# Sliding-window attention and an ELU feed-forward: finer first loads, clears in two steps, another order of the first transfers, and a split last row block

## Chip, cores and metric

The kernel runs on one core of a Trainium2 chip. The metric is the device time of the whole kernel in microseconds (us). The engines are called as in the profile: PE (TensorE, the matrix engine; PEld is its weight load), DVE (VectorE), ACT (ScalarE), POOL (GpSimd) and SP (SyncE). POOL and SP also issue DMA transfers.

## What is computed

The reference takes q, k and v of 8 batches, 8 heads, 576 positions and 64 columns. Each query position attends to the keys at most 32 positions away. The attention output of all heads, 4608 rows of 512 columns, goes through a feed-forward layer with 2048 hidden columns and an ELU between the two matrices.

```python
scores = scale * np.matmul(q, k.transpose(0, 1, 3, 2))       # scale = 1/sqrt(64)
scores = np.where(np.abs(pos[:, None] - pos[None, :]) <= 32, scores, -1e9)
attn = softmax(scores)
x = (attn @ v).transpose(0, 2, 1, 3).reshape(4608, 512)
h = x @ w_in                                                  # 512 -> 2048
g = np.where(h > 0, h, np.exp(np.minimum(h, 0)) - 1)
out = g @ w_out                                               # 2048 -> 512, fp32
```

## The kernel before

Work is cut into 36 **pairs** of 64-row query blocks (i = 0 to 35, 128 rows of x each, 4.5 pairs to a batch) and into 10 **tiles** t of the feed-forward: tiles 0 and 1 hold two pairs (256 rows), the other eight hold four (512 rows). All operations are named, with the engine that does them:

- `L b nm half`: POOL issues a transfer that loads half of the heads of q or k of batch b as bf16 (288 KB). `LV b qb`: the same for a 128-row window of v. `WI c` and `WO c`: a quarter of `w_in` or `w_out` (512 KB). `ID` and `MS` are no transfers: POOL makes the identity matrix and the band masks.
- `T b nm hp` and `E b nm hp` (batches 0 to 2): PE transposes two heads of q or k into PSUM (18 matmuls of 64x64), and ACT copies the result to `qT` or `kT`. In batch 0 DVE does the k copies.
- `SV`: copies within `vw` (`copy_v`) that build the odd windows of v; DVE does them in batches 0 and 1.
- `QK i`, `SM i`, `MK i`, `AV i g`, `RN i g`: scores on PE, exponential on ACT (PSUM `psS`, one buffer), masking on DVE, product with v on PE in two head groups g, normalisation on DVE.
- `XT i` and `X i`: x of pair i is transposed for the feed-forward. Pairs 0 to 7 go over PE (`XT`, 4 matmuls into `psT`) and ACT (`X`, the copy); all later ones are a DMA transpose that SP issues. `psT` has one buffer, which the T of batches 1 and 2 and all XT share. So T, its copy E, XT and its copy X go round one after another, in whatever order PE's queue has them.
- `H t fo` (PE, PSUM `psH` with three buffers), `EX`, `FF`, `GG` (exponential on ACT, then on DVE or ACT, then DVE): one 128-column block of the hidden layer of a tile. `Y t c part` (PE), `YC` (ACT copy), `OUT` (SP transfer): four parts of the second product for 128 output rows.

The order on every engine is written by a planner when the program is built (`class Plan`). Each operation has an engine, an assumed duration, a rank and its dependencies; at each step the engine that is free takes the ready operation of lowest rank. The program that comes out is a fixed queue for each engine: an instruction that waits holds all behind it. POOL's first transfers are an exception, since the list `RING` gives their order by hand. At most eight of POOL's transfers are under way: each one waits for the eighth before it. All of them go through one DMA queue.

Before the plan is run, DVE clears parts of three `vw`, two `kT` and two `pm` buffers (15 memsets), which stand at the head of its queue. The last 128 output rows (tile 9, c = 3) are computed as 16 matmuls of 512 columns; ACT copies one half of the columns and DVE the other, and each half is stored by a transfer of its own.

Of the kernel before, what the change touches and what calls it, by code (L numbers as in the profile page):

```python
# [8 lines left out]
FP32 = mybir.dt.float32  # L9
BF16 = mybir.dt.bfloat16  # L10
# [146 lines left out]
def kernel(  # L157
# [19 lines left out]
    HP = H // 2  # L177
    PR = 96
    TPP = S // PR
    TPW = S // QB  # L180
    NWB = 3
    KW = S + 2 * WIN
# [36 lines left out]
            for b in range(B) for nm in "qk" for hp in range(HP)}  # L219

    def make_masks():
        mf = ep.tile([128, 4, QB], FP32, name="mf", tag="e")
# [26 lines left out]

    def wide(b):  # L250
        return b < NWB

    def load_qk(b, nm, half):
        src = {"q": q, "k": k}[nm]
        src = src[b, half * HP:(half + 1) * HP]
        if half == 0:
            live[nm, b] = bfp.tile(
                [128, HP, TPW * D] if wide(b) else [PR, H, TPP * D], BF16,
                name="bf", tag="bf")
        t = live[nm, b]  # L260
        if wide(b):
            t = t[:, half * HP // 2:(half + 1) * HP // 2]
            src = src.rearrange("(n a) (p t) d -> (a p) n (t d)", a=2, t=TPW)
        else:
            t = t[:, half * HP:(half + 1) * HP]
            src = src.rearrange("h (p t) d -> p h (t d)", t=TPP)
        nc.gpsimd.dma_start(out=t, in_=src)  # L267

    def T(b, nm, hp):
        src = live[nm, b]  # L270
        n = 2 * hp + (nm == "k")
        pool, tag = (psH_p, "psH") if b == 0 and n % 4 else (psT_p, "psT")
        pt = pool.tile([128, TPW, QB] if wide(b) else [128, TPP, PR], BF16,
                       name=tag, tag=tag)
        live["T", b, nm, hp] = pt
        if wide(b):
            for j in range(TPW):
                for a in (0, QB):
                    nc.tensor.transpose(pt[a:a + QB, j, :],  # L279
                                        src[a:a + QB, hp, j * D:(j + 1) * D],  # L280
                                        ident[a:a + QB, a:a + QB])
            return
        for j in range(TPP):
            nc.tensor.transpose(pt[:, j, :],
                                src[:, 2 * hp:2 * hp + 2, j * D:(j + 1) * D],
                                ident[0:PR, 0:PR])

    def E(b, nm, hp):
        pt = live.pop(("T", b, nm, hp))
        if nm == "k":  # L290
            dst = kT[b % NKB][:, hp, WIN:WIN + S]
        else:
            dst = qT[b % NKB][:, hp, :]
        dst = dst.rearrange("c (p t) -> c p t", t=TPW if wide(b) else TPP)
        src = pt.rearrange("c t p -> c p t")
        if EVAC[b, nm, hp] == "ACT":
            nc.scalar.copy(dst, src)  # L297
        else:
            nc.vector.tensor_copy(dst, src)  # L299
# [123 lines left out]
    def X(i):  # L423
# [5 lines left out]
        dst = xts[t][:, :, c * 128:(c + 1) * 128]  # L429
        if i >= NPX:  # L430
            nc.sync.dma_start_transpose(dst, xs)
            return
# [55 lines left out]

    def Y(t, c, part):
        if part == 0:  # L490
            pool, nm = ypool(t, c)
            ys[t, c] = pool.tile([128, DM], FP32, name=nm, tag=nm)
        ps = ys[t, c]
        for fo in range(YQ * part, YQ * part + YQ):
            nc.tensor.matmul(ps, lhsT=gs[t][:, fo, c * 128:(c + 1) * 128],  # L495
                             rhs=w_out_sb[:, fo, :],
                             start=(fo == 0), stop=(fo == NFO - 1))

    def YC(t, c):
        y = yp.tile([128, DM], FP32, name="y", tag="y")  # L500
        if (t, c) == yseq[-1]:
            nc.scalar.copy(y[:, 0:DM // 2], ys[t, c][:, 0:DM // 2])
            nc.vector.tensor_copy(y[:, DM // 2:DM], ys.pop((t, c))[:, DM // 2:DM])
        else:
            nc.scalar.copy(y, ys.pop((t, c)))  # L505
        ys[t, c] = y

    def OUT(t, c):
        r = (tiles[t][0] + c) * 128
        y = ys.pop((t, c))  # L510
        if (t, c) == yseq[-1]:
            nc.sync.dma_start(out[r:r + 128, 0:DM // 2], y[:, 0:DM // 2])
            nc.scalar.dma_start(out[r:r + 128, DM // 2:DM], y[:, DM // 2:DM])
        else:
            nc.sync.dma_start(out[r:r + 128, :], y)

# [11 lines left out]
    YS1 = 2  # L528
    NPX = 8

    P = Plan({"SP": 0.8, "ACT": 0.8, "POOL": 0.8, "DVE": 6.0})
    FC = 512
# [19 lines left out]
    def prank(i):  # L552
        return PER * tiles[where[i][0]][0] + PER * (i - tiles[where[i][0]][0]) - LEAD[i >= NLEAD] - 16

    SVOF = {}
    NV3 = 4
    LQ0, LQD = 64.0, 2.4
    XQ0, XQD = 38.0, 3.0
# [7 lines left out]
        ('L', 0, 'q', 1),  # L566
        ('L', 0, 'k', 1),
        ('ID',),
        ('LV', 0, 0),
        ('LV', 0, 2),  # L570
        ('MS',),
        ('LV', 0, 4),
        ('LV', 0, 6),
        ('WI', 0),
        ('WI', 1),
        ('L', 1, 'q', 0),
        ('L', 1, 'k', 0),
        ('WI', 2),
        ('LV', 0, 8),
        ('WI', 3),  # L580
        ('L', 1, 'q', 1),
        ('L', 1, 'k', 1),
        ('WO', 0),
        ('LV', 1, 0),
        ('WO', 1),
        ('LV', 1, 2),
        ('WO', 2),
        ('LV', 1, 4),
        ('WO', 3),
        ('L', 2, 'q', 0),  # L590
        ('L', 2, 'k', 0),
        ('LV', 1, 6),
        ('LV', 1, 8),
        ('L', 2, 'q', 1),
# [17 lines left out]
    for b in range(B):  # L612
        need = prank(b * NQB // 2)
        for j in range(NTB) if b >= XB else ():
            for nm in "kq":
# [7 lines left out]
                else:  # L623
# [10 lines left out]
                     dma=0.5, wt=0.05, solo=0.4, lat=LATX)  # L634
        for half in range(2) if b < XB else ():
            for nm in ("q", "k"):
                n = ("L", b, nm, half)
                deps = []
                if b >= 2:
                    deps += [("T", b - 2, nm, hp) for hp in range(HP)]  # L640
                P.op(n, "POOL", 0.75, RING.index(n) - 999, deps,
                     lambda b=b, nm=nm, half=half: load_qk(b, nm, half),
                     dma=1.5 if wide(b) else 1.7, wt=0.1, soft=ring(n))
        deps = []
# [3 lines left out]
        for qb in range(0, NQB, 2):  # L648
            x = need - LQ0 + LQD * (qb / 2 + (NV3 if b == XB else 0))
            P.op(("LV", b, qb), "POOL", 0.9,  # L650
                 RING.index(("LV", b, qb)) - 999 if b < XB else x,
                 deps + (gate(x) if b >= XB else []),
                 lambda b=b, qb=qb, g=gate(x) if b >= XB else []: load_v(
                     b, qb, g),
                 dma=1.3 if 0 < qb < NQB - 1 else 1.0, wt=0.04,
                 soft=ring(("LV", b, qb)))
# [15 lines left out]
        for hp in range(HP) if b < XB else ():  # L672
            for nm in ("q", "k"):
                n = hp * 2 + (nm == "k")
                deps = [("L", b, nm, hp // 2), ("ID",)]
                m = n - (4 if b == 0 else 1)
                if m >= 0:
                    deps.append(("E", b, "qk"[m % 2], m // 2))
                elif b:
                    deps.append(("E", b - 1, "k", HP - 1))  # L680
                P.op(("T", b, nm, hp), "PE", 0.5 if wide(b) else 0.3, need - 36 + 4 * n, deps,
                     lambda b=b, nm=nm, hp=hp: T(b, nm, hp))
                deps = [("T", b, nm, hp)]
                if b >= NKB:
# [3 lines left out]
                     lambda b=b, nm=nm, hp=hp: E(b, nm, hp))  # L688

    P.op(("ID",), "POOL", 0.6, RING.index(("ID",)) - 999, [],  # L690
         lambda: make_identity(nc, ident), soft=ring(("ID",)))
# [9 lines left out]
    for i in range(NPAIR):  # L701
# [17 lines left out]
        P.op(("SM", i), "ACT", 1.05, r, deps, lambda i=i: SM(i))  # L719
        deps = [("SM", i), ("MS",)]  # L720
        if i >= 2:
# [28 lines left out]
        if t >= 2:  # L750
            deps.append(("H", t - 2, NFO - 1))
        if i < NPX:
            if i:
                deps.append(("X", i - 1))
# [32 lines left out]
    for n, (t, c) in enumerate(yseq):  # L787
        for part in range(NQ):
            r = (PER * (tiles[t][0] + tiles[t][1])
                 + 2 * YSP.get(t, 1) * (c * NQ + part) + 1)  # L790
            deps = [("GG", t, fo) for fo in range(YQ * part, YQ * part + YQ)]
            deps.append(("WO", part * YQ * NWC // NFO))
            if part:
# [3 lines left out]
            elif c == 1:  # L797
                deps.append(("RN", NPAIR - 1, 1))
            P.op(("Y", t, c, part), "PE", 0.86, r, deps,
                 lambda t=t, c=c, part=part: Y(t, c, part))  # L800
        deps = [("Y", t, c, NQ - 1)]
        if n >= 3:
# [6 lines left out]
    with tc.manual_schedule():  # L809
        for t in vw:  # L810
            nc.vector.memset(t[0:WIN, 0, :, 0:D], 0.0)
            nc.vector.memset(t[128 - WIN:128, NQB - 1, :, 0:D], 0.0)
            nc.vector.memset(t[:, 0:NQB:2, :, D:VW], 1.0)
        for t in kT:
            nc.vector.memset(t[:, :, 0:WIN], 0.0)
            nc.vector.memset(t[:, :, WIN + S:KW], 0.0)
        for t in pm:
            nc.vector.memset(t[:, :, QB:2 * QB], 0.0)
        P.run()
# [28 lines left out]
```

The softmax here doesn't subtract the row's maximum and nothing guards it: scores larger than these inputs give would overflow.

## Time and profile before

| | |
|---|---|
| median of 5 runs | 325.17 us (324.61 to 326.88) |
| the profiled execution's own time | 324.61 us |
| its span | 322.6 us |
| PE busy | 303.9 us (94%) |
| DVE, ACT, POOL busy | 211.6, 196.5, 107.8 us |
| start of the first H (tile 0) | 24.52 us |
| start of the first H of 512 rows (tile 2) | 67.50 us |
| end of PE's last matmul | 318.98 us |

The profiled execution is the fastest of the five, 0.56 us below the median. Its span is the time between the first and the last recorded event; 2.0 us of its time lie around it. An engine's busy time in a slice is the union of its instructions; PE's ends are modelled. In a timeline row the bracket gives how long the engine was idle before the instruction, and what ended that.

### The profile page before, as it was taken

How to read it: one execution, taken by the hardware profiler on the slowest of the kernel's cores; microseconds unless marked ns; L12 is line 12 of the kernel's file. 1: busy time of each engine (PE TensorE's matmuls, PEld its weight loads, DVE VectorE, ACT ScalarE, POOL GpSimd, SP SyncE). 2: the span in 40 equal slices, each digit the busy share in tenths (PEclk: the TensorE clock that was granted, in tenths of full speed). 3: DMA queues.
4: the chain of work that ended last, by engine and by line, in shares of the span. 5: the costliest groups of instructions: out<-in, count | busy, mean ns of one | idle time of the engine just before them, and what ended most of it. 6: DMA issues, size and time to landing. Idle time of an engine off the chain costs nothing.

```text
span 322.6 us, 7515 instructions
## 1 busy us (share of the span) xinstructions
PE 303.9 (94%) x2896; PEld 160.1 (50%) x2896; DVE 211.6 (66%) x500; ACT 196.5 (61%) x333; POOL 107.8 (33%) x203
## 2 busy tenths in 40 slices
PE   1589998899999999999999999999999999999995
PEld 1467666555555444444444444444444454444442
DVE  4586687668888777777666666666666665454500
ACT  3258987778756555555666666666666665556511
POOL 8945447935456645154456434000000000000000
PEclk9999999999999999999999999999999999999999
DMA  7999999999999999999999999532221111000021
GB/s 100 134 203 203 197 196 189 155 169 179 138 148 230 161 170 184 198 142 158 163 131 163 189 150 159 105 83 68 61 60 59 50 53 49 33 35 33 33 98 65
DMA packets 140371, 41.04 MB, mean 127 GB/s; under 512 B 125360, under 2 KB 135856, under 8 KB 140336
## 3 DMA queue, kind: packets, MB, share of 16 engines
q0 software_dynamic: 91872, 18.36, 76.9%
q1 hardware_dynamic: 48320, 22.08, 34.2%
q8 instruction: 22, 0.36, 0.5%
q10 hardware_dynamic: 144, 0.13, 0.1%
q14 instruction: 13, 0.11, 0.1%
HBM read 36.70 MB, written 9.44 MB: 143 GB/s over the span
## 4 chain that ended last, share of the span: by engine, by line
PE 83%; DMA 8%; POOL 4%; ACT 1%; issue 1%; DVE 1%; ACTq 0%; POOLq 0%
PE psH L452 36%; PE psY L495 35%; PE psO L405 5%; DMA vw<-in_v_dram 4%; DMA w_in_sb<-in_moe_w_in_dram 4%; PE psS L372 3%; POOL bf L267 1%; PE psS L495 1%; PE psO L495 1%; PE psT L495 1%; POOL vw L336 1%; PE psT L279 1%; ACT kT L297 1%; POOL w_in_sb L538 0%; PE psT L435 0%
## 5 line engine op out<-in xcount | busy, mean ns | idle before, releaser
L452 PE MATMUL psH<-xt,w_in_sb 128*128 128x512 bf16 (+1 forms) x640 | 148.3, 360 | 0.5 <-DVE g L481 0.5
L460 ACT ACTIVATE e<-psH 128x512 f32<-128x512 f32 (+1 forms) x160 | 88.3, 554 | 88.1 <-PE psH L452 87.4
L495 PE MATMUL psY<-w_out_sb,g 128*128 128x512 bf16 x528 | 134.2, 379 | 0.2 <-DMA w_out_sb<-in_moe_w_out_dram 0.2
L452 PEld LDWEIGHTS <-w_in_sb 128*128 128x128 bf16 x640 | 59.5, 98 | 56.6 <-issue 1.0
L495 PEld LDWEIGHTS <-g 128*128 128x128 bf16 x576 | 52.7, 98 | 56.5 <-issue 0.5
L478 DVE SCALAR_TENSOR_TENSOR g<-f,psH 128x512 bf16<-128x512 bf16 (+1 forms) x72 | 45.0, 624 | 33.9 <-ACT f L470 33.8
L472 DVE TENSOR_SCALAR f<-e 128x512 bf16<-128x512 f32 (+1 forms) x88 | 37.7, 428 | 36.4 <-ACT e L460 36.3
L481 DVE TENSOR_TENSOR g<-psH,f 128x512 bf16<-128x512 f32 (+1 forms) x88 | 56.5, 642 | 3.2
L470 ACT ACTIVATE f<-e 128x512 bf16<-128x512 f32 (+1 forms) x72 | 41.9, 582 | 2.2
L380 ACT ACTIVATE pu<-psS 128x1024 bf16<-128x1024 f32 x36 | 36.7, 1020 | 7.4 <-PE psS L372 6.4
L336 POOL DMA_DIRECT2D vw<-in_v_dram x40 | 33.6, 842 | 15.7 <-issue 3.5
L405 PEld LDWEIGHTS <-pm 128*128 128x128 bf16 x576 | 27.1, 100 | 13.9 <-DVE xs L420 0.5
L308 POOL COPY scr<-g 1x1 bf16<-1x1 bf16 x73 | 14.9, 204 | 53.6 <-DVE g L481 44.1
L420 DVE TENSOR_TENSOR xs<-psO,rc 128x256 bf16<-128x256 f32 x68 | 28.9, 424 | 2.4
L405 PE MATMUL psO<-vw,pm 128*128 128x65 bf16 x544 | 28.4, 195 | 0.3 <-DVE xs L420 0.3
L393 DVE TENSOR_TENSOR pm<-pu,masks 128x512 bf16<-128x512 bf16 x72 | 27.0, 417 | 1.5 <-ACT pu L380 1.5
L317 POOL DMA_DIRECT2D bf<-in_k_dram x25 | 20.9, 838 | 7.3 <-issue 5.2
L317 POOL DMA_DIRECT2D bf<-in_q_dram x25 | 20.9, 838 | 5.2 <-issue 4.1
L505 ACT COPY y<-psY 128x512 f32<-128x512 f32 x33 | 18.8, 570 | 5.3 <-PE psY L495 5.3
L372 PEld LDWEIGHTS <-kT 64*128 64x128 bf16 (+1 forms) x640 | 12.1, 102 | 15.0 <-issue 11.9
L372 PE MATMUL psS<-qT,kT 64*128 64x64 bf16 (+1 forms) x640 | 16.9, 199 | 2.5 <-DVE kT L299 1.4
L418 DVE RECIPROCAL rc<-psO 128x4 f32<-128x4 f32 x68 | 12.3, 181 | 9.9 <-PE psO L405 9.4
(47 smaller groups left out, 99.0 us busy)
## 6 DMA issues: line engine op xcount, KB each, us to landing
out_dram<-y SPq DMA_DIRECT2D x35, 256.0 KB, 2.9
vw<-vw SPq DMA_DIRECT2D x12, 260.0 KB, 7.0
vw<-in_v_dram POOLq DMA_DIRECT2D x24, 128.0 KB, 7.2
bf<-in_k_dram POOLq DMA_DIRECT2D x20, 128.0 KB, 6.7
bf<-in_q_dram POOLq DMA_DIRECT2D x20, 128.0 KB, 6.2
w_in_sb<-in_moe_w_in_dram POOLq DMA_DIRECT2D x4, 512.0 KB, 11.0
w_out_sb<-in_moe_w_out_dram POOLq DMA_DIRECT2D x4, 512.0 KB, 13.9
bf<-in_q_dram POOLq DMA_DIRECT2D x6, 288.0 KB, 10.4
```

Of the source, the lines that this page charges most:

```text
L317: nc.gpsimd.dma_start(out=live["N", nm, b][0:n, j, :].rearrange("p (h d) -> p h d", d=D), in_=src[128 * j:128 * j + n])
L336: nc.gpsimd.dma_start(out=vt[r:r + hi - lo, qb, :, 0:D], in_=vb[lo:hi])
L372: nc.tensor.matmul(psS[p0:p1, h % 2, s, hp, :], lhsT=kT[b % NKB][base:base + 64, hp, c:c + p1 - p0], rhs=rhs, start=True, stop=True)
L380: nc.scalar.activation(pu, live.pop(("S", i)), AX.Exp, scale=SCALE)
L405: nc.tensor.matmul(o[:, j, :], lhsT=p[:, h, s * QB:s * QB + 128], rhs=vw[b % NVB][:, qb, h, :], start=(s == 0), stop=(s == 1))
L452: nc.tensor.matmul(ps, lhsT=w_in_sb[:, do, fo * 128:(fo + 1) * 128], rhs=xts[t][:, do, :], start=(do == 0), stop=(do == NDO - 1))
L460: nc.scalar.activation(e, ps, AX.Exp)
L470: nc.scalar.activation(f, e, AX.Relu, bias=1.0, scale=-1.0)
L472: nc.vector.tensor_scalar(f, e, -1.0, 0.0, ALU.add, ALU.min)
L478: nc.vector.scalar_tensor_tensor(gs[t][:, fo, :], f, -1.0, ps, ALU.mult, ALU.max)
L481: nc.vector.tensor_tensor(gs[t][:, fo, :], ps, f, ALU.max)
L495: nc.tensor.matmul(ps, lhsT=gs[t][:, fo, c * 128:(c + 1) * 128], rhs=w_out_sb[:, fo, :], start=(fo == 0), stop=(fo == NFO - 1))
```

## The change

- **Loads.** q and k of batch 0 come in quarters of the heads (eight transfers of 144 KB) and no longer in halves (four of 288 KB); batches 1 and 2 keep their halves. T of a head pair waits for its own quarter.
- **Clears.** The memsets become operations of the plan: `CL 0` (first `vw`, `kT` and `pm`) at once, `CL 1` (the others) after the first k copy `E 0 k 0`. What uses a buffer waits for its clear.
- **Order of the first transfers.** `RING` is rewritten: ID stands after five quarters, MS after the first `w_in` quarter and not after the second v window; k of batch 1 comes before most of v; the four `w_out` quarters follow each other, and v of batch 1 but for its first window comes after them, in the order 4, 2, 8, 6.
- **Pair 11.** Its x goes over PE and ACT as for pairs 0 to 7.
- **Last rows.** The last row block is computed by column halves (32 matmuls of 256 columns). ACT copies the first half when it is done; of the second, DVE and ACT copy 128 columns each. Three transfers store them.
- Assumed durations of some operations and the times at which the engines are assumed to be free change with it, and with them the planned order on PE, ACT, DVE and SP in the first third of the kernel. Code for a narrow layout of q and k that no batch used is removed.

```diff
-    NWB = 3
+    PARTS = {0: 4, 1: 2, 2: 2}
...
+    def clear(n):
+        for t in vw[:1] if n == 0 else vw[1:]:
+            nc.vector.memset(t[0:WIN, 0, :, 0:D], 0.0)
+            nc.vector.memset(t[128 - WIN:128, NQB - 1, :, 0:D], 0.0)
+            nc.vector.memset(t[:, 0:NQB:2, :, D:VW], 1.0)
+        for t in kT[n:n + 1]:
+            nc.vector.memset(t[:, :, 0:WIN], 0.0)
+            nc.vector.memset(t[:, :, WIN + S:KW], 0.0)
+        for t in pm[n:n + 1]:
+            nc.vector.memset(t[:, :, QB:2 * QB], 0.0)
...
+    def load_qk(b, nm, part):
+        m = PARTS[b]
+        if (nm, b) not in live:
+            live[nm, b] = bfp.tile([128, HP, TPW * D], BF16, name="bf", tag="bf")
+        src = {"q": q, "k": k}[nm][b, part * H // m:(part + 1) * H // m]
+        nc.gpsimd.dma_start(
+            out=live[nm, b][:, part * HP // m:(part + 1) * HP // m],
+            in_=src.rearrange("(n a) (p t) d -> (a p) n (t d)", a=2, t=TPW))
...
     def Y(t, c, part):
+        last = (t, c) == yseq[-1]
...
+        if last:
+            h, n = part // 2, NFO // 2
+            ps = ps[:, h, 0:DM // 2]
+            cols = slice(h * DM // 2, (h + 1) * DM // 2)
+            part %= 2
...
+    def YCL(n, eng, deng):
+        t, c = yseq[-1]
+        r = (tiles[t][0] + c) * 128
+        lo, hi = ((0, 256), (256, 384), (384, 512))[n]
+        y = ep.tile([128, 512], FP32, name="e", tag="e")[:, 0:hi - lo]
+        src = ys[t, c][:, lo // 256, lo % 256:lo % 256 + hi - lo]
+        if eng is nc.scalar:
+            eng.copy(y, src)
+        else:
+            eng.tensor_copy(y, src)
+        deng.dma_start(out[r:r + 128, lo:hi], y)
...
-    NPX = 8
+    NPX = (*range(8), 11)
-    P = Plan({"SP": 0.8, "ACT": 0.8, "POOL": 0.8, "DVE": 6.0})
+    P = Plan({"SP": 0.8, "ACT": 0.8, "POOL": 1.2, "DVE": 1.0})
...
     RING = [
         ('L', 0, 'q', 0), ('L', 0, 'k', 0), ('L', 0, 'q', 1), ('L', 0, 'k', 1),
+        ('L', 0, 'q', 2),
         ('ID',),
+        ('L', 0, 'k', 2), ('L', 0, 'q', 3), ('L', 0, 'k', 3),
         ('LV', 0, 0),
+        ('L', 1, 'k', 0),
         ('LV', 0, 2),
-        ('MS',),
         ('LV', 0, 4), ('LV', 0, 6), ('WI', 0),
+        ('MS',), ('L', 1, 'q', 0),
         ('WI', 1),
-        ('L', 1, 'q', 0), ('L', 1, 'k', 0),
         ('WI', 2), ('LV', 0, 8),
-        ('WI', 3),
         ('L', 1, 'q', 1), ('L', 1, 'k', 1),
+        ('LV', 1, 0), ('WI', 3),
         ('WO', 0),
-        ('LV', 1, 0),
         ('WO', 1),
-        ('LV', 1, 2),
         ('WO', 2),
-        ('LV', 1, 4),
         ('WO', 3),
         ('L', 2, 'q', 0),
+        ('LV', 1, 4),
         ('L', 2, 'k', 0),
+        ('LV', 1, 2), ('LV', 1, 8),
         ('LV', 1, 6),
-        ('LV', 1, 8),
         ('L', 2, 'q', 1), ('L', 2, 'k', 1),
...
+    P.op(("CL", 0), "DVE", 1.5, -999, [], lambda: clear(0))
+    P.op(("CL", 1), "DVE", 3.0, CL1, CLD, lambda: clear(1))   # CL1 = -900, CLD = [("E", 0, "k", 0)]
```

## The prediction, as put on record before the run

> **What bounds the kernel.** I read the table of windows first.
>
> ```profile
> 0.00:8.00 8.00, 1.42 (x46) 1.28 (x48) 4.00 (x15) 2.46 (x3) 6.59 (x18) 1.00 0.71 99
> 8.00:16.00 8.00, 4.30 (x132) 3.58 (x127) 4.44 (x7) 1.94 (x3) 7.62 (x17) 1.00 1.49 133
> 16.00:24.00 8.00, 6.76 (x132) 5.31 (x133) 6.88 (x23) 4.51 (x6) 3.46 (x5) 1.00 1.22 203
> 24.00:32.00 8.00, 7.73 (x128) 6.21 (x129) 4.79 (x15) 6.57 (x16) 4.06 (x5) 1.00 1.32 202
> 32.00:40.00 8.00, 7.86 (x118) 5.40 (x116) 5.53 (x17) 7.54 (x20) 3.33 (x5) 1.00 1.47 197
> ...
> 64.00:300.00 236.00, 236.00 (x1885) 115.34 (x1883) 163.42 (x364) 149.74 (x242) 65.87 (x128) 1.00 1.09 121
> ```
>
> Behind stretch and length stand PE, PEld, DVE, ACT and POOL busy, then the granted clock (1.00 throughout). From 64 to 300 us PE never idles: only what lies before, and the tail, can move the end.
>
> To see what PE loses I price its work by the pieces of the chain of waits: T 0.40, QK 0.42 (0.34 or 0.47), AV 0.25, XT 0.385, H of 256 rows 0.44, H of 512 rows and a Y part 0.865. With the counts 24, 36, 72, 8, 32, 128 and 144 that makes 295.2 us. PE ends at 318.98: 23.8 are lost. At the first wide H (67.50) 43.7 us of the queue are done, lost 23.8 again, so nothing is lost after it. At H(0,0) (24.52) 7.55 are done, lost 17.0; at QK 4 (40.43) 20.8, lost 19.6. The three losses: 17.0, 2.6, 4.2.
>
> PE's timeline shows the third:
>
> ```profile
> 52.72 0.38 PE L435 MATMUL psT<-ident,xs 128*128 128x128 bf16 x4 [1.29 <-ACT kT L297]
> 58.27 0.38 PE L435 MATMUL psT<-ident,xs 128*128 128x128 bf16 x4 [0.73 <-ACT kT L297]
> 63.44 0.38 PE L435 MATMUL psT<-ident,xs 128*128 128x128 bf16 x4 [0.43 <-ACT kT L297]
> 67.50 1.90 PE L452 MATMUL psH<-xt,w_in_sb 128*128 128x512 bf16 x8
> ```
>
> An XT right behind a T in PE's queue stands until ACT has emptied the one psT. Starts in these rows lie apart: T to its E 0.52, E to XT 0.69, XT to X 0.45, X to the next T 0.63 (T to E and XT to X 0.1 to 0.2 more before 25 us).
>
> Start and end, from the timelines of POOL, DVE and ACT:
>
> ```profile
> 10.02 0.40 POOL L247 CAST masks<-mf 128x256 bf16<-128x256 f32 x1
> 13.78 0.76 DVE L299 COPY kT<-psH 128x576 bf16<-128x576 bf16 x1
> 16.37 0.76 DVE L393 TENSOR_TENSOR pm<-pu,masks 128x512 bf16<-128x512 bf16 x2 [0.92 <-ACT pu L380]
> 20.14 0.59 ACT L441 COPY xt<-psT 128x512 bf16<-128x512 bf16 x1
> 319.05 0.37 ACT L502 COPY y<-psS 128x256 f32<-128x256 f32 x1 [2.87 <-PE psS L495]
> 319.45 0.42 DVE L503 COPY y<-psS 128x256 f32<-128x256 f32 x1 [13.15 <-ACT y L502]
> 319.91 0.37 ACTq L513 DMA_DIRECT2D out_dram<-y  x1
> ```
>
> The masks are ready at 10.42, long before the first masking (16.37). The last k copy, 13.78, holds QK 0. In the tail DVE's copy waits for ACT's.
>
> **Quarters.** By their issues and times to landing the halves land at 5.43, 7.74, 9.64 and 11.54, then v window 0 at 12.50 and window 2 at 13.34. For a quarter: q 0 lands between 3.3 and 5.4 (half a transfer earlier, or no earlier); I take 4.5, then 0.97 each, half of 1.9 to 2.0, so k 3 at 11.3. Its ends: 10.0, where its issue (ending near 7.5) plus 2.5 sets it, and 15, if a transfer cannot come faster than 1.5 after the one before. Windows of 96 and 128 KB follow each other by 0.96 and 0.84, so I stay at 0.97.
>
> The Trainium skill ("DMA: Bandwidth & Descriptors", section "Anatomy of one DMA — SWDGE (gpsimd) path") speaks against this change: each transfer costs about 2.0 us plus its bytes over 436 GB/s. Added up, eight quarters would cost by it some 18.7 us against 10.7 for four halves, and the sum 8 us more; the 0.84 between two landings says that the fixed part overlaps in a queue.
>
> **Clears.** 5 us of memsets leave the head of DVE's queue (1.6 stay, beside the first loads). The other 3.3 (two vw at 1.42, kT 0.2, pm 0.27) now stand behind the first k copy: that runs 6.75 to 7.5, the clear to 10.8, k copies 1 and 2 to 12.2. The next instruction, a v copy, waits for window 0 (11.3 + 0.96 = 12.25) and ends at 12.85; the last k copy runs to 13.6, QK 0 to 14.25. Before it was 15.2: 0.9 earlier. A k 3 at 10.0 would gain little more, since DVE is busy until 12.2 either way.
>
> **Order of transfers.** That 0.9 is lost again. An issue takes 0.70 at 256 rows, 0.76 at 512, 0.87 at 1024, so a quarter some 0.67. Five quarters and ID end at 5.45 (ID ended at 4.86); three quarters, v 0, k of batch 1, three v windows and `w_in` 0 bring POOL to 12.35; MS takes its 3.95 as before and ends at 16.3, now the last to come for MK 0: 16.35, as before. ACT's queue now has all four SM before X 0: SM starts come 1.9 apart (psS has one buffer), so SM 3 ends at 21.1 and X 0 starts there, against 20.14. Then T(1,q,0) 21.75, E 22.3, XT 1 23.0, X 1 23.55, T(1,k,0) 24.2, H(0,0) 24.9. q of batch 1, issued behind MS, lands near 21, in time. One more T is done by then: 24.9 less 7.95 is 17.0 lost. First loss: no change.
>
> **Second loss.** PE's new queue has XT 2 right behind T(1,q,1) and XT 3 right behind T(1,q,2), with two EX and one FF before the E on ACT: PE stands twice for 1.2 (26.2 to 27.4, 30.95 to 32.15). Before it had H between them. Step by step this gives QK 4 at 39.15 with 19.1 us done: lost 20.1, 0.5 more. On the other side ACT (6.57 and 7.54 of 8) is nearly full here and has one E (0.54) less left at 24.9: 0.5 less. I take 0.2 more, nearer to the steps.
>
> **Third loss.** The new queue has an XT right behind a T only at XT 5 and XT 6: 0.85 each; T(2,k,0) waits 0.2, XT 4 0.05; the rest has 1.1 us or more of Y and H in between. 1.95 instead of 4.2: 2.25 less. What could be late: with MS gone from between the v windows the queue's hole (13.34 to 15.17, where 0.85 is usual) closes. With the landing distances of before (W 2.2 to 2.6, half 1.4, v 0.9) `w_out` 3 lands at 42.3 (was 46.19), q of batch 2 at 43.7 (was 47.61), but v window 2 of batch 1 at 47.5 (was 40.63). Its reader AV 5 now stands behind Y(0,1,1), at 52. Cover: 4 us. Bounds of this term: nothing, if other waits fill the place, and 3.
>
> **Pair 11.** Four matmuls more on a full PE: 0.385. The ACT copy (0.59) lies beside, and SP's transpose (1.37) was covered: issued at 86.7, 5.0 to landing, and H(3,0) came at 93.9.
>
> **Last rows.** 32 matmuls of 256 columns at 0.11: 3.52 against 3.46, so 0.05. The first half's copy is hidden. Of the second, DVE copies 128 columns (0.31, from 0.42 at 256) and ACT's copy (0.26) waits for it in the built program, as DVE waited for ACT before. 0.07 + 0.31 + 0.03 + 0.26 + 0.04 against 0.07 + 0.37 + 0.03 + 0.42 + 0.04: 0.2 less; 0.55 if they ran side by side.
>
> **Sum.** 0 + 0.2 - 2.25 + 0.385 + 0.05 - 0.2 = -1.8. The profiled execution took 324.61, so 322.8; the same on the median, 325.17, is 323.4. 0.5% (1.6 us, so 323.54) is about what a measurement of this kernel can tell from no change; the sum lies just beyond it.
>
> **Rivals.**
> - *The early waits cost nothing* (18%). ACT sets the second stretch, the steps before H(0,0) take no more than the later ones (0.4), the tail's copies run side by side: 0.2 + 0.5 + 0.4 + 0.35 below the sum, 321.9. For it: ACT's 7.54 of 8.
> - *The ladder only moves* (15%). The waits that leave the third loss come back at other places, the 2.25 shrink to 0.8: 324.8. For it: every psT step is still there. Against: eight gaps in PE's queue are wide enough.
> - *A quarter costs nearly as much as a half* (12%), the slow side. At 1.2 us per quarter k 3 lands at 13.0 and 1.7 of the sum are gone; at 1.5 it lands at 15, and the last k copy, QK 0, the four SM and X 0 all come 3.7 later than assumed: 327.1. It decides from 1.2 on. For it: the first halves took 1.9 to 2.3, those of batch 1 1.4, so something slows the start that I can't name.
> - *The change doesn't do what it says*: the side-by-side copies of the last half do wait for each other; it is in the sum.
>
> **How the numbers follow.** The forecast holds 55%, 322.4 to 324.6 by the bounds of the second and third loss; seven tenths of it lie below 323.54. With the 18% that makes 0.57 faster; the rest of it and the moved ladder make 0.31 same; the slow case 0.12 slower. The range leaves out the tip of the first rival and the slow one: 321.2 to 325.8.
>
> **What would show it.** Right: landings of quarters about 1 us apart; MS ending near 16.3 and MK 0 right behind; H(0,0) near 24.9; PE idle over 1 us before XT 2 and XT 3; under 2.5 us of PE idle from 40 us to the first wide H, and that near 67.1 with 45.4 us of work done; a full PE behind it. Wrong: k 3 later than 13; DVE standing at a copy of v near 48; PE idle after 68, or before XT 11.

## The result, and the profile after

The changed kernel takes 326.41 us in the median of 53 runs, the kernel before 325.08 in the median of 95 runs: a ratio of 1.0024, with a 95% interval of 1.0013 to 1.0035. That is a quarter of a per cent slower where half a per cent faster was predicted. The ratio is taken without the executions in a slower state that either kernel falls into now and then (six of the kernel before, at 328.9 to 332.5 us, and three of the changed one), and it is not the ratio of the two medians, which is 1.0041. The median hides something: the times of the changed kernel fall into two groups, 21 runs below 325.6 and 31 above 326. Of the kernel before only 18 of 95 are above 326.

The profiled execution took 326.62 us, its span 324.9 (before: 324.61 and 322.6), so the 2.3 us to be explained are those of the span. The table of windows has the same columns as before: stretch, length, PE, PEld, DVE, ACT and POOL busy, granted clock, DMA.

```profile
16.00:24.00 8.00, 5.76 (x114) 5.02 (x114) 6.65 (x22) 4.72 (x6) 6.67 (x9) 1.00 1.21 193
24.00:32.00 8.00, 7.13 (x86) 5.24 (x85) 2.69 (x8) 4.12 (x9) 3.77 (x5) 1.00 1.42 198
32.00:40.00 8.00, 6.80 (x118) 5.26 (x116) 5.69 (x17) 6.57 (x16) 2.55 (x3) 1.00 1.24 206
...
64.00:300.00 236.00, 235.45 (x1898) 116.17 (x1898) 166.11 (x373) 149.56 (x244) 65.36 (x127) 1.00 1.06 119
```

From 64 us on PE is full, as before (235.45 of 236). What is new lies in the two rows from 24 to 40 us. PE looks busy there (7.13 and 6.80 of 8), but in the first row it got only 86 matmuls done where the kernel before had 128, and DVE and ACT had 2.69 and 4.12 us of work instead of 4.79 and 6.57. A busy engine that delivers less is slower per instruction. PE's timeline shows it (start, duration, then the group of matmuls with their count, and in brackets how long PE stood and for whom):

```profile
25.09 1.90 PE L448 MATMUL psH<-xt,w_in_sb 128*128 128x256 bf16 x8
26.92 0.69 PE L280 MATMUL psT<-ident,bf 64*64 64x64 bf16 x18
28.43 0.59 PE L431 MATMUL psT<-ident,xs 128*128 128x128 bf16 x4 [0.83 <-ACT qT L293]
28.81 2.77 PE L448 MATMUL psH<-xt,w_in_sb 128*128 128x256 bf16 x12
31.51 0.69 PE L280 MATMUL psT<-ident,bf 64*64 64x64 bf16 x18
...
33.62 0.47 PE L280 MATMUL psT<-ident,bf 64*64 64x64 bf16 x18
35.13 0.38 PE L431 MATMUL psT<-ident,xs 128*128 128x128 bf16 x4 [1.05 <-ACT qT L293]
```

Eight matmuls of 256 columns take 1.90 us at 25.09, and the next group starts 1.83 later: about 0.23 from start to start. In the profile before eight such matmuls took 1.05 at 30.85, and the next group started 0.88 later, 0.11 each:

```profile
23.89 0.69 PE L279 MATMUL psT<-ident,bf 64*64 64x64 bf16 x18 [0.23 <-ACT xt L441]
...
27.16 0.47 PE L279 MATMUL psT<-ident,bf 64*64 64x64 bf16 x18
...
30.85 1.05 PE L452 MATMUL psH<-xt,w_in_sb 128*128 128x256 bf16 x8
```

T takes 0.69 in the new profile at 26.92 and at 31.51, and 0.47 only from 33.62 on. So PE's matmuls run at half rate, and they come to full rate at about 33 us. In the profile before the same two rates can be seen, but the change comes at about 26.6 (T of 0.69 at 23.89, of 0.47 at 27.16).

The column of the granted clock says 1.00 in all these rows and can't show this. It is an average over the throttle's own entries in the trace (its array `0/clock`), and time without an entry counts as full. The first entry is one of full clock that begins at 33.18 us in the new profile and at 26.63 in the one before, the moments at which the durations change; there is none for the time ahead of it. Behind PE's last matmul there is an entry of 0.50, which the column does show (the 0.88):

```profile
318.00:325.00 7.00, 3.13 (x28) 2.40 (x25) 0.29 (x1) 0.78 (x3) 0.00 (x0) 0.88 0.22 75
```

So the half rate goes with the clock. That the clock was 0.50 ahead of the first entry is not recorded; it is read from matmuls that take twice as long.

The start and the third loss went nearly as the prediction had them. The start, from several engines:

```profile
12.61 0.76 DVE L295 COPY kT<-psH 128x576 bf16<-128x576 bf16 x1
...
14.78 0.40 POOL L258 CAST masks<-mf 128x256 bf16<-128x256 f32 x1
...
15.79 0.29 DVE L349 COPY vw<-vw 64x520 bf16<-64x520 bf16 x1 [0.16 <-DMA vw<-in_v_dram]
...
16.42 0.76 DVE L389 TENSOR_TENSOR pm<-pu,masks 128x512 bf16<-128x512 bf16 x2
...
20.72 0.59 ACT L437 COPY xt<-psT 128x512 bf16<-128x512 bf16 x1
```

The last k copy ends at 13.37, the masks at 15.18, X 0 starts at 20.72. The third loss, and the first wide H:

```profile
59.66 0.38 PE L431 MATMUL psT<-ident,xs 128*128 128x128 bf16 x4 [0.73 <-ACT qT L293]
...
64.34 0.38 PE L431 MATMUL psT<-ident,xs 128*128 128x128 bf16 x4 [0.73 <-ACT qT L293]
...
70.99 1.25 PE L448 MATMUL psH<-xt,w_in_sb 128*128 128x512 bf16 x5
```

And the tail:

```profile
317.31 2.78 PE L499 MATMUL psS<-w_out_sb,g 128*128 128x256 bf16 x24
...
320.13 0.37 ACT L520 COPY e<-psS 128x256 f32<-128x256 f32 x1 [1.99 <-PE psS L499]
...
320.55 1.03 PE L499 MATMUL psS<-w_out_sb,g 128*128 128x256 bf16 x8 [0.46 <-ACT e L520]
...
321.69 0.29 DVE L522 COPY e<-psS 128x128 f32<-128x128 f32 x1 [13.43 <-PE psS L499]
322.02 0.27 ACT L520 COPY e<-psS 128x128 f32<-128x128 f32 x1 [1.51 <-DVE e L522]
```

Here is a wait that the sum did not have: PE's last eight matmuls stand 0.46 us until ACT has copied the first column half (0.37 at 320.13).

By the prediction's own accounts (time less work done):

| term | predicted | first profile | a_look2 (below) |
|---|---|---|---|
| first loss, to H(0,0) | 0 | +0.2 | +0.1 |
| second, to QK 4 | +0.2 | **+3.3** | +0.3 |
| third, to the first wide H | -2.25 | -1.7 | -1.8 |
| pair 11 and the halves | +0.44 | +0.44 | +0.44 |
| PE's wait for the first half's copy | none | +0.46 | +0.46 |
| tail after PE's end | -0.2 | -0.3 | -0.3 |
| sum | -1.8 | +2.4 | -0.8 |

For the second row: H(0,0) at 25.09 with 7.95 done, QK 4 at 42.18 with 19.08 done, so 17.1 and 23.1 lost; 6.0 between them, where the kernel before had 2.7. The sum of 2.4 is the span's 2.3.

### The profile page after: what moved, and what is told of

It is laid out like the page before. It is cut to its first block, busy times and chain, and to the rows that moved or that the text cites. A ratio compares the mean times of both kernels' runs of the same rounds, so it can differ in the third digit from the quotient of the medians.

```text
span 324.9 us, 7555 instructions
## 1 busy us (share of the span) xinstructions
PE 306.0 (94%) x2916; PEld 163.9 (50%) x2916; DVE 210.5 (65%) x500; ACT 197.3 (61%) x335; POOL 109.7 (34%) x207
## 4 chain that ended last, share of the span: by engine, by line
PE 87%; ACT 5%; POOL 2%; DMA 2%; DVE 2%; issue 1%; DVEq 0%; ACTq 0%; POOLq 0%
PE psH L448 38%; PE psY L499 35%; PE psO L401 5%; PE psS L368 3%; DMA vw<-in_v_dram 2%; POOL bf L268 2%; PE psT L280 1%; PE psS L499 1%; ACT e L456 1%; PE psT L499 1%; PE psO L499 1%; ACT qT L293 1%; PE psT L431 1%; ACT pu L376 1%; DVE pm L389 1%
## 5 line engine op out<-in xcount | busy, mean ns | idle before, releaser
L448 PEld LDWEIGHTS <-w_in_sb 128*128 128x128 bf16 x640 | 60.7, 99 | 57.9 <-issue 0.4
L499 PEld LDWEIGHTS <-g 128*128 128x128 bf16 x592 | 53.9, 98 | 54.5 <-issue 0.6
```

Source lines behind the costliest of these rows:

```text
L448: nc.tensor.matmul(ps, lhsT=w_in_sb[:, do, fo * 128:(fo + 1) * 128], rhs=xts[t][:, do, :], start=(do == 0), stop=(do == NDO - 1))
```

## The experiments

The main theory was that the holes which the new order leaves before XT 2 and XT 3 delay the moment at which PE's matmuls reach full rate. The rival was that the copies on ACT and DVE (the ladder T, E, XT, X) set this stretch whatever PE's rate. In the runs below the moment of full rate is that of the first entry of full clock in the trace, or of the first group of matmuls (a T of 0.47 us in most) with full-rate durations; the two agree to within one group of matmuls.

**Fillers in the one hole (a_fill_gap).** A helper issues matmuls that nothing reads:

```diff
+    def fill(pool, tag, n, cols):
+        w = pool.tile([128, 512], FP32, name=tag, tag=tag)[:, 0:cols]
+        for _ in range(n):
+            nc.tensor.matmul(w, lhsT=ident, rhs=qT[0][:, 0, 0:cols], start=True, stop=True)
...
+        if i == 2:                      # in X(i), ahead of its transposes
+            fill(psS_p, "psS", 4, 256)
```

> The changed kernel with four 256-column matmuls more on TensorE, into an idle psS, between T(1,q,1) and XT 2, where TensorE stood 0.83 us. Theory 'late full rate': TensorE runs its matmuls at half rate until it has been fed without a gap for some 4 us, and this gap at 27.6 us starts the count again; with it filled, the 512-row-equivalent rate (0.13 us for a 256-column matmul, from 0.23) comes at about 28.5 us and not at 33.2, the 5.4 us of half-rate work after 28.8 shrink by some 1.8 us, QK 4 comes at about 40.4 and not 42.2, time about 324.6. Rival 'the ladder of copies': ScalarE's and VectorE's copies bound this stretch, the rate of TensorE does not matter; the fillers change nothing or cost 0.1, time 326.3 to 326.6.

Measured: 324.37 (322.91 to 326.02; ratio to before 0.9975, 0.9949 to 1.0002), one of 12 runs above 326. The time is what the main theory said, and the interval lies below that of the changed kernel (1.0013 to 1.0035). The profile is weaker than it looks: the full rate was there at 27.26, ahead of the fillers at 27.66, so this one execution would have been early without them. It is the spread of the times that speaks here.

**Fillers at the head only (a_fill_head, b_fill_head).** Three 512-column matmuls behind QK 0 and two behind QK 1, in the changed kernel and in the one before.

```diff
         live["S", i] = psS              # in QK(i)
+        if i in {0: 3, 1: 2}:
+            fill(psH_p, "psH", {0: 3, 1: 2}[i], 512)
```

> The changed kernel with five 512-column matmuls more on TensorE in its idle time behind QK 0 (three) and QK 1 (two). 'Late full rate': TensorE is fed from 13.4 to 18.8 us, full rate comes at about 18 and stays; T, AV and XT before 25 us fall to 0.47, 0.41 and 0.38 and H to 0.13 a matmul, H(0,0) comes up to 0.5 earlier, QK 4 about 3 us earlier (39.2), time about 323.4. Rival 'ladder of copies': the same holes, only longer; 326.2 to 326.6. If the gaps of 0.2 to 0.7 us after 21 us take the rate away again, it is as the plain changed kernel.

> The kernel before with the same five matmuls behind QK 0 and QK 1. 'Late full rate': it runs at half rate only to about 26.5 us, so it has less to win: some 0.7 us between 24.5 and 26.5 and up to 0.5 before H(0,0); time 324.0 to 324.5. Rival 'ladder of copies': 325.0 to 325.3.

Measured: 326.17 (ratio 1.0018, 0.9991 to 1.0045), eight of 12 above 326, full rate in the profile at 33; and 325.14 (1.0003, 0.9979 to 1.0027), full rate at 19.6. The first is a miss for the main theory as it was put: PE had no hole above 0.33 from 14.3 to 22.1, and this did not bring the rate; the holes of 0.67 and 0.83 behind it were still there. The second says that an early full rate alone is worth little to the old order, as the rival had it: its first wide H came at 67.09, 0.4 earlier, and the time did not move.

**The late parts undone (a_old_end).** Same order, with x of pair 11 by SP's transpose and the old code for the last rows:

```diff
+        if i == 11:                     # in X(i)
+            live["XT", i] = (dst, xs)
+            return
...
+        if i == 11:                     # in XE(i): pt is xs here
+            nc.sync.dma_start_transpose(dst, pt)
+            return
...
-        last = (t, c) == yseq[-1]       # in Y; copies and transfers as before
+        last = False
```

> The changed kernel with x of pair 11 by SP's transpose again and the last rows' matmuls, copies and DMAs as in the kernel before; all the rest, order included, as changed. By the prediction's terms (pair 11 0.385, halves 0.05, tail -0.2) 0.2 less; by the trace after (0.46 us in which TensorE waits for ScalarE's copy of the first half, which that sum did not have) 0.7 less: 325.7. If these parts cost nothing, 326.4.

Measured: 325.37 (1.001, 0.9986 to 1.0034). From the first wide H to PE's end it takes 249.72 us, the changed kernel 250.59: 0.87 less, where pair 11 (0.385), halves (0.05) and the wait (0.46) make 0.90. What follows PE's end is 3.68, against 3.32. So these parts cost 0.5 net, and the expectation of 0.7 had left out that last gain. The median is 1.0 below the changed kernel's; between two groups of times a median of 12 runs can't weigh half a us. Its profile also gave the first hint at chance: the queue is the changed kernel's, but the full rate came at 27.8, and the first wide H 43.3 us behind H(0,0) where the first profile has 45.9.

**The holes taken out by order (a_move).** The plan's order is kept, and single operations are moved before they are issued:

```diff
+MOVES = [                               # each first one goes right behind the second
+    (("XT", 2), ("H", 0, 3)), (("X", 2), ("EX", 0, 3)),
+    (("T", 1, "k", 1), ("AV", 3, 1)), (("E", 1, "k", 1), ("EX", 0, 4)),
+    (("XT", 3), ("H", 0, 7)), (("X", 3), ("EX", 0, 7)),
+    (("T", 1, "k", 2), ("H", 0, 9)), (("E", 1, "k", 2), ("EX", 0, 9)),
+    (("T", 1, "q", 3), ("H", 0, 11)), (("E", 1, "q", 3), ("EX", 0, 11)),
+    (("T", 1, "k", 3), ("H", 0, 13)), (("E", 1, "k", 3), ("EX", 0, 13))]
```

> The changed kernel with the same work, but XT 2 and XT 3 moved on TensorE (and X 2, X 3 on ScalarE) behind two more H, and the next T and E of batch 1 behind one or two H each, so that no XT stands right behind a T before 42 us. The first four runs fell in two groups by when the matmuls double their rate (27 or 33 us). 'Holes delay the full rate': TensorE is fed without a gap from 24.0 us on, so full rate comes by 31 us in every run, and the holes of 0.83 and 1.05 are gone too: QK 4 at 39.5 to 40.3 (42.18 in the changed kernel), median 323.0 to 324.3, no run over 326. Rival 'ladder of copies': ScalarE paces the stretch, the holes come back before other T and H, QK 4 at 41 to 42, 325.5 to 326.4.

Measured: 324.54 (0.997, 0.9944 to 0.9996), none of 12 above 326. Full rate came at about 28.7 (eight matmuls of H from 27.55 take 1.60), QK 4 at 39.27. The ladder did not bring the holes back: from H(0,0) to QK 4 PE stood 0.19 us where it had stood 1.88. Part of the gain was lost later (third loss 3.0): PE stood 0.84 us at QK 8, with no releaser that the profile names.

**Fillers in all holes (a_fill_all).** The helper of a_fill_gap at five places:

```diff
+        if i < 2:                       # in QK(i), at its end
+            fill(psH_p, "psH", 4, 256)
...
+        if i in {2: 4, 3: 6}:           # in X(i), ahead of its transposes
+            fill(psS_p, "psS", {2: 4, 3: 6}[i], 256)
...
+        if i == 1:                      # in X(i), behind its transposes
+            fill(psS_p, "psS", 3, 256)
```

> The changed kernel in its order with filler matmuls of 256 columns in every hole from 14 to 35 us: four behind QK 0 and QK 1, three behind XT 1, four before XT 2, six before XT 3. The five fillers of the head alone moved the time by only 0.2 us, those before XT 2 alone by 2.0. 'Holes delay the full rate': fed from 13.4 us on with no gap over 0.3, full rate comes by 21 us, at the latest by 28; the holes as such stay, so 323.8 to 324.6 and no run over 326. If activity of TensorE has no part in it, 326.2 to 326.6 and both groups of runs.

Measured: 324.02 (0.9947, 0.992 to 0.9974), none of 12 above 326, full rate at 25.4. As expected, though not as early as 21.

**The mirror, first try (b_hole).** In the kernel before:

```diff
+MOVES = [(("XT", 2), ("T", 1, "k", 0)), (("X", 2), ("E", 1, "k", 0))]
```

> The mirror: the kernel before with XT 2 moved right behind T(1,k,0) (and X 2 behind its copy), which puts a hole of some 0.8 to 1.2 us at about 27.6 into an order that had none there. 'Holes delay the full rate': part of the runs now change rate only at 31 to 34 us and take 2 us more; median 326.0 to 327.5, two groups. Rival 'a hole costs what it is long': 325.2 to 326.2 in one group; 'ladder of copies': 325.2.

Measured: 325.26 (1.0006, 0.9984 to 1.0027). A miss, and the profile says why: T took 0.47 at 26.01, the hole of 0.73 came at 26.5, behind the change of rate (25.2). There the hole cost nothing that 12 runs can tell: the interval reaches from 0.5 us less to 0.9 more.

**The tail in two tiles (a_tail).** The second column half goes into its own PSUM tile.

```diff
+                ys[t, c] = [ys[t, c], psH_p.tile([128, DM], FP32, name="psH", tag="psH")]
...
-            ps = ps[:, h, 0:DM // 2]
+            ps = ps[h][:, 0:DM // 2]
```

> The changed kernel with the second column half of the last rows in its own psH tile and not in one psS tile with the first: TensorE no longer waits for ScalarE's copy of the first half. The wait of 0.46 us at 320.1 goes, all else the same: 325.9 (0.46 less). If the copy of the first half is late for another reason, 326.4.

Measured: 325.86, still in two groups (five runs at 323.7 to 324.6, seven at 325.9 to 326.6). PE no longer stands at 319: from the first wide H to PE's end 249.98 instead of 250.59. So the wait was for the shared tile.

**Fillers in the earlier hole (a_fill_24).** Three 256-column matmuls behind XT 1, nothing else.

```diff
         live["XT", i] = (dst, pt)       # in X(i), behind its transposes
+        if i == 1:
+            fill(psS_p, "psS", 3, 256)
```

> The changed kernel with three 256-column fillers behind XT 1 alone, where TensorE stands 0.67 us at 23.4; the hole of 0.83 at 27.6 stays. If the full rate needs a stretch of some 3.4 us without a hole, which may begin anywhere, TensorE is now fed from 21.6 to 27.6 us and full rate comes by 28 us in most runs: median 324.3 to 325.0, few runs over 326. If only the hole at 27.6 counts: 326.0 to 326.5, two groups.

Measured: 324.15 (0.9971, 0.9947 to 0.9996), one of 12 above 326. PE's timeline:

```profile
23.31 0.84 PE L422 MATMUL psS<-qT,ident 128*128 128x256 bf16 x3
24.19 0.69 PE L280 MATMUL psT<-ident,bf 64*64 64x64 bf16 x18
...
25.18 1.04 PE L456 MATMUL psH<-xt,w_in_sb 128*128 128x256 bf16 x8
26.15 0.47 PE L280 MATMUL psT<-ident,bf 64*64 64x64 bf16 x18
```

The fillers at 23.31 close the hole ahead of T(1,k,0); that T is still at half rate, and the eight matmuls of H at 25.18 take 1.04 where the first profile of the changed kernel has 1.90. Three matmuls that compute nothing are worth 2.3 us between the medians, and 1.7 by the ratios to the kernel before (0.9971 against 1.0024, with intervals that don't meet). Most of it is that late executions became rare.

**The mirror, holes ahead of the change (b_hole2).** In the kernel before:

```diff
+MOVES = [
+    (("T", 1, "k", 0), ("T", 1, "q", 0)), (("E", 1, "k", 0), ("E", 1, "q", 0)),
+    (("T", 1, "q", 1), ("H", 0, 2)), (("E", 1, "q", 1), ("EX", 0, 2)),
+    (("T", 1, "k", 1), ("T", 1, "q", 1)), (("E", 1, "k", 1), ("E", 1, "q", 1))]
```

> The mirror again, with holes ahead of the doubling: the kernel before with T(1,k,0) right behind T(1,q,0), and T(1,q,1) and T(1,k,1) right behind H(0,2) and each other; each second T stands until the one psT is empty, some 0.7 us at 24.5 and again at 28 to 29. 'Holes delay the full rate': median 326.0 to 327.5, part of the runs change rate after 30 us. Rival 'a hole costs at most its length': 325.2 to 325.9 and one group.

Measured: 327.22 (1.0064, 1.0042 to 1.0086), all seven runs above 326. PE's timeline:

```profile
28.65 0.69 PE L293 MATMUL psT<-ident,bf 64*64 64x64 bf16 x18
30.08 0.69 PE L293 MATMUL psT<-ident,bf 64*64 64x64 bf16 x18 [0.73 <-ACT qT L311]
30.70 2.74 PE L466 MATMUL psH<-xt,w_in_sb 128*128 128x256 bf16 x12
...
36.13 0.47 PE L293 MATMUL psT<-ident,bf 64*64 64x64 bf16 x18
```

Two holes of 0.73 us (at 24.2 and here at 29.3) make T stay at 0.69, and 12 matmuls of H take 2.74; full rate comes at about 34, and the time is 2 us longer. The mirror now shows what the changed kernel showed, in the order of before.

**Quarters undone (a_halves).** Each half is issued at the place of its first quarter:

```diff
+        if m == 4:                      # in load_qk
+            if part % 2:
+                return
+            part, m = part // 2, 2
```

> The changed kernel with q and k of batch 0 in halves again, each half issued at the place of its first quarter, all else as changed. The prediction's first loss: the start is set by the masks and by ScalarE's queue, not by the last k copy, so H(0,0) within 0.4 of 25.1 and the time 326.2 to 326.8. Rival 'quarters bring the start forward': H(0,0) 0.6 to 1.0 later and 327.0 to 327.4. If each quarter's own issue costs more than it brings, 325.5.

Measured: 327.26 (1.0059, 1.0026 to 1.0091). The second k half lands at 11.36, as the last quarter did in the first profile (11.34). The first line is of the first profile of the changed kernel, the others of this run:

```profile
11.34 0.75 PEld L280 LDWEIGHTS <-bf 64*64 64x64 bf16 x18 [0.67 <-DMA bf<-in_k_dram]
...
11.36 1.08 PEld L284 LDWEIGHTS <-bf 64*64 64x64 bf16 x37 [1.20 <-DMA bf<-in_k_dram]
...
13.26 0.69 PE L284 MATMUL psH<-ident,bf 64*64 64x64 bf16 x18 [0.73 <-ACT qT L297]
```

But the copies of the last heads then bunch: the last T of k waits for a PSUM buffer, until ACT has copied a q, and starts at 13.26 and not 11.53, the last k copy at 14.09 and not 12.61, QK 0 ends 1.5 later, and H(0,0) starts at 26.57 against 25.0 to 25.9 in the profiles of the changed kernel. So by this one profile the quarters do bring the start forward, by 0.7 to 1.6 us; my expectation, that they bring nothing in the new order of transfers, was wrong. The time alone can't show it, since its interval meets that of the changed kernel.

**The changed kernel itself, three more profiles (a_look2, a_look3, a_look4).** No edit.

> The changed kernel itself once more, for one profile: is the moment at which its matmuls double their rate a property of the run? If 'holes delay the full rate' is right, the same program shows it at 27 to 28 us in some executions and at 32 to 35 in others, and the first wide H follows: about 45.9 us after H(0,0) when late (as in the first profile), about 43.3 when early, the time 326 to 327.5 or 324.4 to 325.3. If the moment is fixed by the program, it is 33.0 again.

> As the look before: late (32 to 35 us) with 45.0 to 46.0 from H(0,0) to the first wide H and 326 to 327.5, or early (27 to 28) with 43.3 and 324.4 to 325.3; what would speak against it is an early change with a long time, or the reverse.

> As the two looks before: the time follows the moment of the change of rate, 43.3 us from H(0,0) to the first wide H with an early one and 45.0 to 46.0 with a late one.

Measured, with the two earlier profiles that have this order:

| profile | first entry of full clock | first T at full rate | H(0,0) to first wide H | second loss | span | own time |
|---|---|---|---|---|---|---|
| a_look2 | 21.99 | 22.1 | 42.8 | 3.0 | 321.7 | 323.49 |
| a_old_end (other end) | 27.84 | 27.8 | 43.3 | 3.8 | 322.7 | 325.57 |
| a_look3 | 32.45 | 32.3 (in part, 0.51) | 45.0 | 5.3 | 324.8 | 326.48 |
| first profile | 33.18 | 33.6 | 45.9 | 6.0 | 324.9 | 326.62 |
| a_look4 | 33.87 | 34.4 | 45.4 | 5.9 | 325.1 | 326.83 |

One and the same program takes 323.5 or 326.8, and the time follows the moment of full rate. The time of a_old_end lies 2.9 us above its span, where the others' lie 1.7 to 1.8 above; by its span, and with the 0.5 for its cheaper end, it stands between a_look2 and the late ones. Of a_look2:

```profile
24.34 0.47 PE L280 MATMUL psT<-ident,bf 64*64 64x64 bf16 x18 [0.67 <-ACT xt L437]
...
25.00 1.03 PE L448 MATMUL psH<-xt,w_in_sb 128*128 128x256 bf16 x8
25.96 0.47 PE L280 MATMUL psT<-ident,bf 64*64 64x64 bf16 x18
27.48 0.38 PE L431 MATMUL psT<-ident,xs 128*128 128x128 bf16 x4 [1.05 <-ACT qT L293]
```

T is at 0.47 already at 24.34, and eight matmuls of H take 1.03; the hole before XT 2 (1.05) is there and longer than in the first profile, but nothing is left for it to delay.

**All of it together (a_best).** The changed kernel with eleven fillers (four behind QK 0 and QK 1, three behind XT 1), the moves of a_move and the same for XT 5 and XT 6, the tail in two tiles, pair 11 on SP.

```diff
+    (("XT", 5), ("Y", 1, 0, 0)), (("X", 5), ("XT", 5)),     # more MOVES
+    (("T", 2, "k", 2), ("AV", 6, 1)), (("E", 2, "k", 2), ("EX", 1, 9)),
+    (("XT", 6), ("Y", 1, 0, 1)), (("X", 6), ("FF", 1, 11)),
+    (("T", 2, "k", 3), ("H", 1, 12)), (("E", 2, "k", 3), ("EX", 1, 12))
```

> What the runs so far point to, put together on the changed kernel: seven H-sized fillers of the head (four 256-column matmuls behind QK 0 and QK 1, three behind XT 1) so that the full rate comes before 28 us, XT 2, 3, 5 and 6 moved away from the T in front of them, the second half of the last rows in a psH tile, x of pair 11 by SP's transpose again. From the fillers alone (first wide H at 67.84) less the holes left there (0.51, 0.29 and twice 0.73) the first wide H at 65.6 to 66.5; 249.8 us of work behind it and 3.3 of tail and 1.7 around the span: 320.4 to 321.3. If the holes only move, as the ladder of copies would have it, 322.5 to 323.5.

The fillers are eleven matmuls of 256 columns, not seven. Measured: 321.76 in the median of six (320.42 to 322.15), a ratio to the kernel before of 0.9892 (0.9868 to 0.9916); its profile took 320.59. First wide H at 65.92, PE's end at 315.68, both as expected; the profiled execution lies in the expected range of times, the median 0.5 us above it. From H(0,0) to there PE stood 0.51 us in all, where it had stood 3.71. This version beats both kernels.

## Why the prediction was wrong, point by point

- **First loss, no change: right in its size, half right in its working.** Quarters landed 0.96 us apart (first T at 4.6, k 3 at 11.34; taken: 4.5 and 11.3). H(0,0) came at 25.09 (taken: 24.9). The masks were ready at 15.18 and not 16.3, since an issue of a quarter took 0.55 and not 0.67; the last thing ahead of MK 0 (16.42) was instead a v window, for whose copy DVE waited until 15.79. That the quarters' 0.9 is lost again to the masks was not so: without quarters H(0,0) came 0.7 to 1.6 later (a_halves). What in the new order takes it back is not shown.
- **Second loss, +0.2: this is the step that failed.** The holes were there as predicted (0.83 and 1.05 for 1.2 each). But I priced all PE work at its full-rate durations, and so the time that the kernel before spends at half rate sat unseen in its second loss of 2.6, where I took it for a constant. It is not: it depends on the holes ahead of it. At the prices of the first profile the work between 25.1 and 33.3 takes 3.5 us more than at full rate (five H at 0.475, and T, XT and AV the rest), in the kernel before some 1.1 us: this is 2.4 of the 3.1 that the term was off; 0.3 more is what I took off the steps' 0.5 on ACT's account; the 0.4 that remain are not accounted for. The sign was in the timeline of before, T of 0.69 at 23.89 and of 0.47 at 27.16. With an early full rate the step's own working holds: QK 4 was taken for 39.15 and came at 39.10 in a_look2 (with holes of 1.05 for 1.2, and H(0,0) 0.1 later).
- **Third loss, -2.25: right in mechanism.** XT 5 and XT 6 waited 0.73 each (taken: 0.85), T(2,k,0) 0.16; the term came out as -1.7 and -1.8, and -2.0 to -2.2 in a_look3, a_look4 and a_old_end. Behind the first wide H PE was full.
- **Pair 11, halves, tail.** 0.385 and 0.05 are borne out by a_old_end, the tail gained 0.3 (taken: 0.2). What was missed is PE's wait of 0.46: I saw that DVE and ACT wait for each other over one PSUM tile, and not that PE, which goes on writing the same tile, does too.
- **The rivals.** None was it. The early waits cost nothing: no, they cost most. The ladder only moves: no, in a_best the holes went and stayed away. A quarter nearly as dear as a half: no, and that its 327.1 lies near the typical time is chance. A rival on the rate of matmuls was not among them, since the clock's column read 1.00; that column is blind ahead of its first entry.

The Trainium skill ("TensorE: Matmul & The Clock Gate", Part 1) says that the array runs at half rate until it has been busy for about 3.4 us, as judged in windows that run freely and not from the kernel's start, and that the number of slow matmuls differs from run to run. The runs here agree on these points: half-rate and full-rate durations and nothing lasting in between, the change at 22 to 34 us in one program, and earlier or later on the whole when holes are filled or made. The page also says that the ramp costs below 1% of a typical kernel, and that one should not fit to a count of slow matmuls; here an early and a late change lie 0.9 to 1% apart in time (a_look2 against a_look3 and a_look4), and that decides the sign.

The traces show the windows themselves. In all 17 profiles the entry of full clock lasts a whole number of steps of 3.413 us: 85 of them (290.13 us) in the first profile, 87 (296.96) in the kernel before, 88 (300.37) in a_look2, 85 to 89 in the rest. So both changes of the clock lie on a grid of that step, and the grid lies differently against the kernel's start in each execution of one program (the first entries of the changed kernel, 21.99, 32.45, 33.18 and 33.87, are not whole steps apart). That is at least part of the chance in the times. It would also explain why a short hole can cost more than its length: a window that the hole spoils is followed by another one at half rate, 3.41 us in which up to 1.7 us of work is lost (an estimate: half of the step). In the first profile the window from 26.36 to 29.77 holds the hole of 0.83, with PE busy for 2.58 us; in the next PE is busy for all 3.41, and at its end the clock comes.

What stays open is what counts as busy. Feeding PE from 14 to 22 us, mostly by 64-column and 65-column matmuls, did not do it (a_fill_head), and closing the 0.67 at 23.4 alone did. PE's busy share does not decide it: 2.88 us were enough in a_fill_gap (the window from 23.84 to 27.25, much of it 256-column matmuls), 3.01 in a_fill_head (19.49 to 22.90) and 3.10 in the kernel before (19.81 to 23.22) were not.

## What to carry to other kernels

Read PE's speed from the durations of equal matmuls along the timeline, not from its busy share, and not from the clock's column ahead of the throttle's first entry; a price list made at one rate hides what is lost at the other. While PE is still at half rate, a hole of 0.7 to 0.8 us can cost more than its length (by the ratios, some 1.4 times in b_hole2, 1.9 in a_fill_gap and 2.6 in a_fill_24), and a few matmuls that compute nothing, or a better place for a waiting one, can save it; behind the change of rate no hole of these runs was seen to cost more than itself. When a kernel's times lie in two groups, take profiles of the same program until both are seen.

## What was not expected of the hardware

- One program reaches full matmul rate anywhere from 22 to 34 us, with 3.3 us between its shortest and longest profiled time; the column of the granted clock reads 1.00 in all of these stretches, since the throttle's entries begin only with full clock.
- The full clock lasts a whole number of steps of 3.413 us in every profile, 85 to 89.
- Once at full rate, holes of 1.05 us (a_look2 at 27.48, the first profile at 35.13) did not bring half rate back: the next XT took 0.38, and the entry of full clock runs on past PE's end.
- Two transfers of 144 KB can land as fast as one of 288 KB: the last k landed at 11.34 in quarters and at 11.36 in halves, in one profile each.
- Three matmuls of 256 columns with no use brought 2.3 us between medians, 1.7 by the ratios.
